# Single-chunk blocks at the start of a recurrence that is interleaved with a mixture of experts, and first weights in two tiles

## The chip, the cores and the metric

One core of one Trainium2 chip, fp32 throughout. The metric is the device time of one execution in microseconds (us). The median of three runs of the kernel before was 1271.88 us (1271.21 to 1275.32).

## The reference

A recurrence over 768 steps for 4 x 8 heads of width 40, whose output is the input of a mixture of four experts for every token.

```python
for t in range(S):                       # S = 768, state is (B, H, 40, 40)
    y[:, :, t] = einsum('bhd,bhde->bhe', r_t, state)
    Sa = einsum('bhde,bhe->bhd', state, a_t)
    state = state * w_t[:, :, None, :] - einsum('bhd,bhe->bhde', Sa, b_t)
    state = state + einsum('bhd,bhe->bhde', v_t, k_t)
x = y.transpose(0, 2, 1, 3).reshape(B * S, H * D)      # 3072 tokens x 320
p = domain_probs / domain_probs.sum(-1, keepdims=True)
out = sum(p[:, e:e + 1] * (relu(x @ w1[e]) @ w2[e]) for e in range(4))   # 320 -> 1024 -> 320
```

## The kernel before: the parts that matter

The 768 steps are 12 chunks of 64. Chunks are grouped into blocks: [0], then [1,2], [3,4] and so on to [9,10], then [11]. Within a block the recurrence is made parallel: both halves of the batch are prepared (transposes, running products, the `pef` products), one solve on VectorE inverts all small triangular systems of the block at once, then a chain of small products gives the block's output `Yo`. `AE` is the operand that VectorE prepares for `pef`; `pi` and `px` are the first products after the solve and need its results F and XT; `py` are the last ones before `Yo`. The mixture of a finished block is put into a queue of pieces, and TensorE works on those pieces in the gaps of the next block's recurrence. TensorE's order is fixed by the program: a call `mix(n)` stands where pieces may run, and the `credit` spreads the queue over the block.

```python
def mix(us):
    credit[0] += us * credit[1]
    while queue and credit[0] >= queue[0][0] / 2:
        t, piece = queue.pop(0)
        credit[0] -= t
        piece()

def attention(b, after):
    for p in range(NP):
        ...                                    # prepare half p, up to the pef products
        mix((22, 12)[p])
        ...
        mix(4.3)
        ...
    solve()                                    # VectorE; its last steps write F, then XT
    ...
    mix(40)                                    # pieces meant to run during the solve
    for x in range(2):
        for u in us:
            last = inverse(u, x)               # pi needs F, px needs XT
        ...
        mix(4.3)
    ...                                        # the chain to py and Yo, with more mix calls

for y, b in enumerate(all_blocks):
    credit[:] = [0.0, (sum(t for t, _ in queue) - 17) / 124]
    attention(b, ...)
    credit[:] = [sum(t for t, _ in queue) - 17, 1.0]
    mix(0)                                     # 17 us of pieces are left for the next block
    queue += mixture(b.cs, b.xT)
```

A piece is `wide` (hidden units: `ph` products, then ReLU on ScalarE) or `narrow` (`po` products, then a weighted sum into `osb` on VectorE).

```python
def mbank(name):
    return ps.tile([P, 512], FP32, name=name, tag="mbank", bufs=4)

def wide(e, f):
    ph = [mbank("ph") for _ in range(2)]
    ...
def narrow(e, tt):
    po = mbank("po")
    ...                                        # 8 products of 320 columns
    nc.vector.scalar_tensor_tensor(            # tensor_scalar for the first expert
        out=osb[tt][:], in0=po[:, 0:DM], scalar=sc, in1=osb[tt][:], op0=ALU.mult, op1=ALU.add)
```

The order of VectorE's instructions is chosen by the tile framework's scheduler when the kernel is built, except where `tc.issue_after` ties it.

## Time and profile before

The tables below cut the trace at the moments where the second `Yo` of a block starts. "Idle" is wall less busy time of TensorE (PE).

| stage of the kernel before | until | wall us | PE busy | PE idle |
|---|---|---|---|---|
| block [0] | 84.5 | 84.5 | | |
| block [1,2] | 226.8 | 142.3 | 108.6 | 33.7 |
| block [3,4] | 419.2 | 192.4 | 184.6 | 7.8 |
| the rest | 1270.0 | 850.8 | 823.3 | 27.5 |

From block [3,4] on TensorE is the bound; before, it often waits for VectorE.

### The profile page before, as it was taken

How to read it: one execution, taken by the hardware profiler on the slowest of the kernel's cores; microseconds unless marked ns; L12 is line 12 of the kernel's file. 1: busy time of each engine (PE TensorE's matmuls, PEld its weight loads, DVE VectorE, ACT ScalarE, POOL GpSimd, SP SyncE). 2: the span in 40 equal slices, each digit the busy share in tenths (PEclk: the TensorE clock that was granted, in tenths of full speed). 3: DMA queues.
4: the chain of work that ended last, by engine and by line, in shares of the span. 5: the costliest groups of instructions: out<-in, count | busy, mean ns of one | idle time of the engine just before them, and what ended most of it. 6: DMA issues, size and time to landing. Idle time of an engine off the chain costs nothing.

```text
span 1270.0 us, 28505 instructions
## 1 busy us (share of the span) xinstructions
PE 1153.0 (91%) x12736; PEld 785.1 (62%) x12736; DVE 710.6 (56%) x953; ACT 277.7 (22%) x588; POOL 80.4 (6%) x120
## 2 busy tenths in 40 slices
PE   3268679989999998999998999998999999999998
PEld 2256658756567656567656557655558656566776
DVE  7979865878513868604778704569903546601000
ACT  2112332032141032141122141122231212131111
POOL 5000000100000000000000000000000000000110
PEclk9768779998999998999998999998999999999999
DMA  6537444874323574333555424465314472232453
GB/s 135 126 84 156 105 105 96 179 178 102 98 49 95 120 176 108 86 84 95 119 151 107 114 63 103 99 165 112 93 46 86 110 160 49 77 84 74 120 150 93
DMA packets 164633, 138.21 MB, mean 109 GB/s; under 512 B 78688, under 2 KB 148384, under 8 KB 164512
## 3 DMA queue, kind: packets, MB, share of 16 engines
q0 software_dynamic: 17600, 73.46, 23.2%
q1 hardware_dynamic: 144192, 62.13, 22.6%
q8 instruction: 100, 1.64, 0.6%
q10 hardware_dynamic: 2720, 0.82, 0.3%
q14 instruction: 21, 0.17, 0.0%
HBM read 128.50 MB, written 7.86 MB: 107 GB/s over the span
## 4 chain that ended last, share of the span: by engine, by line
PE 66%; DVE 21%; DMA 6%; issue 4%; SPq 1%; ACT 1%; DVEq 0%; POOL 0%; ACTq 0%
PE po L594 24%; PE ph L582 24%; DVE KNT L209 3%; DVE GI L259 3%; PE py L496 2%; PE pc L484 2%; DMA out_dram<-osb 2%; PE pef L294 2%; PE pVST L429 2%; PE py L524 2%; PE pt L468 2%; DVE AT L209 2%; DVE tmp L360 2%; PE pa L458 2%; PE pSN L429 1%
## 5 line engine op out<-in xcount | busy, mean ns | idle before, releaser
L582 PE MATMUL ph<-xT,w1s 64*128 64x512 f32 (+1 forms) x2240 | 437.1, 538 | 11.5 <-DMA xT<-yD 8.1
L594 PE MATMUL po<-w2s,hs 128*128 128x320 f32 x1536 | 434.9, 443 | 0.5 <-ACT hs L588 0.5
L594 PEld LDWEIGHTS po<-w2s,hs 128*128 128x128 f32 x1536 | 294.1, 194 | 134.2 <-issue 20.2
L582 PEld LDWEIGHTS ph<-xT,w1s 64*128 64x128 f32 x2240 | 221.2, 190 | 198.4 <-issue 182.7
L588 ACT ACTIVATE hs<-ph 128x512 f32<-128x512 f32 (+1 forms) x224 | 110.1, 534 | 625.4 <-PE ph L582 624.8
L603 DVE SCALAR_TENSOR_TENSOR osb<-po,gate,osb 128x320 f32<-128x320 f32 x72 | 38.5, 547 | 218.1 <-PE po L594 217.9
L259 DVE RECIPROCAL GI<-G 128x512 f32<-128x512 f32 x24 | 78.6, 3309 | 0.1
L568 POOL DMA_DIRECT2D w1s<-in_moe_w_dram x56 | 37.8, 679 | 628.1 <-PE ph L582 628.0
L475 DVE TENSOR_SCALAR VS__98<-pt 64x320 f32<-64x320 f32 x12 | 5.8, 481 | 121.8 <-PE pt L468 121.8
L301 ACT COPY F<-pef 32x512 f32<-32x512 f32 x96 | 45.1, 470 | 110.6 <-PE pef L294 109.2
L572 POOL DMA_DIRECT2D w2s<-in_moe_w_dram x28 | 26.0, 928 | 532.9 <-PE po L594 525.5
L294 PE MATMUL pef<-AE__111,KNT 40*64 40x64 f32 x640 | 20.3, 310 | 31.9 <-DVE AE__111 L277 31.9
L435 DVE COPY VST<-pVST 128x512 f32<-128x512 f32 x24 | 16.6, 692 | 46.4 <-PE pVST L429 46.3
L294 PE MATMUL pef<-AE__110,KNT 40*64 40x64 f32 x896 | 18.8, 240 | 24.1 <-DVE AE__110 L277 24.1
L294 PEld LDWEIGHTS pef<-AE__111,KNT 40*64 40x64 f32 x640 | 18.8, 218 | 35.0 <-issue 35.0
L360 DVE TENSOR_TENSOR tmp<-Y,Tl 128x1024 f32<-128x1024 f32 (+2 forms) x49 | 35.7, 729 | 1.7
L406 PE MATMUL pi<-F 32*32 32x32 f32 x768 | 15.6, 203 | 23.1 <-DVE F L383 23.1
L364 DVE TENSOR_REDUCE Xl<-tmp 128x32 f32<-128x128 f32 (+3 forms) x49 | 35.5, 725 | 1.7
L364 DVE TENSOR_REDUCE Y<-tmp 128x32 f32<-128x256 f32 (+3 forms) x49 | 35.5, 725 | 1.7
L294 PEld LDWEIGHTS pef<-AE__110,KNT 40*64 40x64 f32 x896 | 17.0, 152 | 29.6 <-DVE AE__110 L277 22.6
L315 PE MATMUL pkn<-ident,KNT 128*128 128x128 f32 x192 | 30.0, 303 | 3.8 <-DVE AE__110 L303 3.1
L490 DVE TENSOR_TENSOR CX<-pc,mask 128x512 f32<-128x512 f32 x48 | 29.9, 684 | 6.1 <-PE pc L484 6.1
(120 smaller groups left out, 1050.7 us busy)
## 6 DMA issues: line engine op xcount, KB each, us to landing
w1s<-in_moe_w_dram POOLq DMA_DIRECT2D x56, 640.0 KB, 8.3
w2s<-in_moe_w_dram POOLq DMA_DIRECT2D x28, 1280.0 KB, 7.2
xT<-yD SPq DMA_DIRECT2D x24, 320.0 KB
yD<-Yo SPq DMA_DIRECT2D x48, 80.0 KB
out_dram<-osb SPq DMA_DIRECT2D x48, 80.0 KB
nat__76<-in_w_dram SPq DMA_DIRECT2D x16, 160.0 KB
nat__76<-in_a_dram SPq DMA_DIRECT2D x16, 160.0 KB
nat__74<-in_r_dram SPq DMA_DIRECT2D x16, 160.0 KB
```

The lines of the kernel that those rows point to most:

```text
L209: nc.vector.transpose(out=out.rearrange("p c m (r q) -> p m q c r", q=nq), in_=n[:, Q:Q + end].rearrange("p (m q e) -> p m q e", q=nq, e=D ...
L259: last = nc.vector.reciprocal(out=b.GI[:, c], in_=b.G[:, c, :, 1:L + 1])
L294: nc.tensor.matmul(out=pef[s][half(x), m * L:(m + 1) * L], lhsT=KNT[rows(s), m, x, :], rhs=u.AE[rows(s), s, m, :], start=True, stop=True,)
L301: nc.scalar.copy(out=F_[r, u.m, 0:L - z * Q], in_=cut(pef[s][r])[:, :, z * Q:L])
L360: nc.vector.tensor_tensor(out=m, in0=in0[:, :, None, :].to_broadcast([P, n0, n1, nr]), in1=in1[:, None, :, :].to_broadcast([P, n0, n1, nr] ...
L364: nc.vector.tensor_reduce(out=out, in_=m, axis=AX.X, op=ALU.add, negate=negate)
L429: nc.tensor.transpose(out=p[:, j * P:(j + 1) * P], in_=t[:, i, j].rearrange("p s d -> p (s d)"), identity=ident[:],)
L568: nc.gpsimd.dma_start(out=w1s[half(d)], in_=moe_w1[e, :, d * (F // 2):(d + 1) * (F // 2)].rearrange("(k p) f -> p k f", p=64),)
L582: nc.tensor.matmul(out=ph[d][:, 0:n], lhsT=w1s[half(d), k_, f * P:(f + 1) * P], rhs=xT[half(d), k_, 0:n], start=(k_ == 0), stop=(k_ == NK ...
L588: nc.scalar.activation(out=hs[-1][1][:, 0:n], in_=ph[d][:, 0:n], func=ACTF.Relu)
L594: nc.tensor.matmul(out=po[:, 0:DM], lhsT=h[:, tt * P:(tt + 1) * P], rhs=w2s[:, f, :], start=(x == 0), stop=(x == NF - 1),)
L603: nc.vector.scalar_tensor_tensor(out=osb[tt][:], in0=po[:, 0:DM], scalar=sc, in1=osb[tt][:], op0=ALU.mult, op1=ALU.add,)
```

## The change

The idle time of TensorE is in the first blocks, where there is little mixture to fill it. With single chunks at the start, [0], [1], [2], the mixture of chunk 1 is ready earlier and can fill block [2]. A larger part of the queue (30 us for 17) is carried into the first block of two. The first expert weights `w1s` are held in two tiles of half the columns each, so that one can be refilled earlier. Chunk 0's clearing of `XT` is remembered as the end of the solve for VectorE's order.

```diff
             if by is nc.vector:
-                by.memset(XT[o, :, 0:Q], 0.0)
+                last = by.memset(XT[o, :, 0:Q], 0.0)
 ...
+        return last.ins
 ...
-            w1s = wts.tile([P, NK, F // 2], FP32, name="w1s", tag="w1s", bufs=1)
+            w1s = [wts.tile([P, NK, F // 4], FP32, name=f"w1s{x}", tag=f"w1s{x}", bufs=1) for x in range(2)]
 ...                                # four DMAs of half the columns for two
-            mix((22, 12)[p])
+            mix(((11, 8), (22, 12))[b.n - 1][p])
 ...
-            cleared(nc.vector)
+            solved.append(cleared(nc.vector))
 ...
-    all_blocks = [block(cs) for cs in [[0]] + [[c, c + 1] for c in range(1, NC - 1, 2)] + [[NC - 1]]]
+    all_blocks = [block(cs) for cs in [[0], [1], [2]] + [[c, c + 1] for c in range(3, NC - 1, 2)] + [[NC - 1]]]
 ...
-        credit[:] = [0.0, (sum(t for t, _ in queue) - 17) / 124]
+        left = 17 if y + 1 == len(all_blocks) or all_blocks[y + 1].n <= b.n else 30
+        credit[:] = [0.0, (sum(t for t, _ in queue) - left) / (85, 124)[b.n - 1]]
 ...
-        credit[:] = [sum(t for t, _ in queue) - 17, 1.0]
+        credit[:] = [sum(t for t, _ in queue) - left, 1.0]
```

More of the change, by code (lines that the diff above doesn't have):

```diff
@@ L392, in cleared @@
             if by is nc.vector:
-                by.memset(XT[o, :, 0:Q], 0.0)
+                last = by.memset(XT[o, :, 0:Q], 0.0)
             else:
-                by.copy(out=XT[o, :, 0:Q], in_=zero[o, None, :].to_broadcast([Q, 2 * NP * M, Q]))
+                last = by.copy(out=XT[o, :, 0:Q], in_=zero[o, None, :].to_broadcast([Q, 2 * NP * M, Q]))
+        return last.ins
     def inverse(u, x):
@@ L560, in weights @@
         def weights(e):
-            w1s = wts.tile([P, NK, F // 2], FP32, name="w1s", tag="w1s", bufs=1)
+            w1s = [wts.tile([P, NK, F // 4], FP32, name=f"w1s{x}", tag=f"w1s{x}", bufs=1) for x in range(2)]
             w2s = wts.tile([P, NF, DM], FP32, name="w2s", tag="w2s", bufs=1)
             if cs[0] == e == 0:
-                for t in (w1s, w2s):
+                for t in w1s + [w2s]:
                     nc.gpsimd.tensor_copy(out=t[:, 0, 0:1], in_=all_blocks[0].units[1].KNT[:, 0, 0, 0:1])
-            for d in range(2):
-                nc.gpsimd.dma_start(
-                    out=w1s[half(d)],
-                    in_=moe_w1[e, :, d * (F // 2):(d + 1) * (F // 2)].rearrange("(k p) f -> p k f", p=64),
-                )
+            for x in range(2):
+                for d in range(2):
+                    o = (2 * d + x) * (F // 4)
+                    nc.gpsimd.dma_start(
+                        out=w1s[x][half(d)], in_=moe_w1[e, :, o:o + F // 4].rearrange("(k p) f -> p k f", p=64),
+                    )
             nc.gpsimd.dma_start(out=w2s[:], in_=moe_w2[e].rearrange("(f p) d -> p f d", p=P))
@@ L582, in wide @@
                     nc.tensor.matmul(
-                        out=ph[d][:, 0:n], lhsT=w1s[half(d), k_, f * P:(f + 1) * P], rhs=xT[half(d), k_, 0:n],
+                        out=ph[d][:, 0:n], lhsT=w1s[f // 2][half(d), k_, f % 2 * P:(f % 2 + 1) * P], rhs=xT[half(d), k_, 0:n],
                         start=(k_ == 0), stop=(k_ == NK - 1),
```

## The prediction

> **What bounds the kernel now.** I read the page first (busy shares, slices), then the table of busy time by stretch, with the stretches cut where VectorE starts a new block, then TensorE's waits in the first stretches, then the timeline of the second block.
>
> ```profile
> PE   3268679989999998999998999998999999999998
> DVE  7979865878513868604778704569903546601000
> PEclk9768779998999998999998999998999999999999
> ```
>
> TensorE is full from slice 7 on (a slice is 31.75 us); VectorE is full before that. The table says how much there is to win (columns: wall, then busy us of PE, PEld, DVE, ACT, POOL, then granted clock, DMA share, GB/s):
>
> ```profile
> 0.00:88.00 88.00, 36.42 (x752) 32.86 (x752) 72.47 (x117) 14.91 (x32) 18.90 (x39) 0.84 0.51 109
> 88.00:236.00 148.00, 117.57 (x1878) 97.96 (x1880) 109.95 (x143) 36.61 (x86) 6.83 (x9) 0.82 0.53 119
> 236.00:430.00 194.00, 186.48 (x2102) 123.31 (x2099) 115.30 (x147) 47.30 (x98) 10.47 (x14) 0.97 0.49 117
> 430.00:624.00 194.00, 185.07 (x2072) 120.61 (x2072) 111.23 (x145) 43.85 (x90) 7.75 (x10) 0.98 0.45 106
> ```
>
> Rows: block [0], block [1,2], then two of the four full blocks of two. PE is idle 51.6 us in [0], 30.4 in [1,2], 8 to 9 in each later one. Block [1,2] has only the mixture of chunk 0 to fill TensorE with, and runs at a granted clock of 0.82. The change aims there. TensorE's waits in 88:236 and the timeline name the cause:
>
> ```profile
> PE pef L294 <- DVE AE__111 L277: 13.2, 2, 12.5
> PE pi L406 <- DVE F L383: 8.8, 1, 8.8
> PE ph L582 <- DMA xT<-yD: 8.1, 2, 7.7
> ```
> ```profile
> 92.20 1.19 PE L582 MATMUL ph<-xT,w1s 64*128 64x256 f32 x2 [7.74 <-DMA xT<-yD]
> 106.21 0.33 PE L294 MATMUL pef<-AE__110,KNT 40*64 40x64 f32 x4 [1.39 <-DVE AE__110 L277]
> 135.83 0.48 PE L294 MATMUL pef<-AE__111,KNT 40*64 40x64 f32 x4 [12.46 <-DVE AE__111 L277]
> 175.54 3.62 PE L406 MATMUL pi<-F 32*32 32x32 f32 x128 [8.75 <-DVE F L383]
> ```
>
> So block [1,2] is a VectorE chain: ready at 89.2, first half prepared at 106.2, second at 135.8, solve done at 175.5; then a mixed chain to the last py product at 226.7. The same landmark of block [3,4] is 419.1. After that every block is bound by TensorE with about 17 us of mixture left over, before and after the change alike. **The whole question is whether the last py of [3,4] comes before or after 419.1.**
>
> **What the Trainium skill says.** "TensorE: Matmul & The Clock Gate", Part 1: a TensorE idle for about 3.4 us falls to half clock, and needs as long to recover. The trace agrees: the 16 po products at 110.3 took 7.05 us, 4.47 at 118.9. "VectorE: DVE Perf Modes", The TRN2 errata: each instruction pays a fixed latency, so two small ones cost more than a large one. It agrees for products (686 ns for 512 columns, 1220 for 1024), not for transposes (about 690 ns for 512, 1980 for 1024): one-chunk blocks have the cheaper transposes. "DMA: Bandwidth & Descriptors", Anatomy of one DMA: about 2 us plus bytes/436 GB/s, so 1280 KB would be some 5 us; this trace has 7.2 to 8.3 us to landing. The trace decides.
>
> **The change part by part.**
>
> *Costs added.* One more block means one more solve: 31.0 to 64.9 in block 0, 33.9 us of VectorE whatever the block's size. It means one more pass over the expert weights (73.46 MB / 7 = 10.5 MB). And 512 columns of mixture become two times 256: a ph group of 20 costs 2.36 us at 256 against 4.35 at 512, so 16 x (4.72 - 4.35) = 6 us, plus group edges; I use 8.
>
> *Block 0* gets shorter: the clears of XT go ahead of the R transposes (about 1 us of the pt wait), and the next decay is one chunk, not two (transpose 0.71 for 1.97, scans 1.2 for 2.3), in the way of the VS copies. I take 2 us: VectorE free at 87.2, xT at 90.2.
>
> *Block [1].* The queue counts a wide piece at 2.15 and a narrow one at 4.3, 68.8 in all, so (68.8-17)/85 = 0.61 us of mixture per unit. 11 units: 3 wide pieces, cold, 10 us, to 100.2 (the AE is ready near 96). pef 2, a wide and a cold narrow piece 9.4, pkn 1.1: 112.8; the second AE is ready at about 112 (masks 4, GI 3.3, transposes 2.1, products 2 after the first). pef and masks to 118, R 0.7, solve to F 29.9 (block 0: 31.0 to 60.9), three osb rows 1.6: F at 150. TensorE has 35 us of work in that time: it fits. From F: pi and px 2.4, pt 2.1, VST to py 9.35 (192.5 to 201.85), mixture 17.2 x 0.61 x 1.07 = 11.2: last py at **175**.
>
> *Block [2].* VectorE: 4.8 after py (as 226.7 to 231.5), G 2.0, GI 3.3, transposes 2.1, products 1.9: pef at 189. TensorE has 11 x 0.66 x 1.07 = 7.7 us ready, so it waits 6. Second AE 12 later, 201; masks 4, R, solve and osb 32.2: F at 237.5; TensorE gets to it at 240. Tail 13.8 + 12.1: last py at **266**. So a one-chunk block takes 90 us, a VectorE chain again, against 78 to 82 us of TensorE work in it.
>
> *Block [3,4].* Its mixture is 68.8 + 30 carried, (98.8-17)/124 = 0.66 per unit; block [1,2] had (68.8-17)/124 = 0.42, the full blocks 1.11. So it is the former [1,2] over again: VectorE ready at 270.8, G 4.4, then 136.5 (89.3 to 226.7 less 0.9 for the gates): 411.7. More mixture after the solve: (0.66-0.42) x 34.4 x 1.07 = 8.9. A warmer TensorE gives back about 4 (pef 3.7 against 2.1, pi 3.6 against 2.2, VectorE's waits on them). Loads in the dense one-chunk blocks cost about 3 on VectorE's path: the fourth load is issued only after the gather. Last py: 411.7 + 8.9 - 4 + 3 = **419.6**, against 419.1.
>
> *Split w1s tile.* Waits on w1s are 2.0 us in all now (longest 0.8); it saves at most that, and mainly keeps the added 256-column mixtures from stalling: the first half can be refilled two wide pieces earlier.
>
> Sum: 1271.9 + 0.5 = 1272.4. The new constants (30, 11, 8, 85) look fitted on a chip, which is no measurement but makes me lean a little to gain: I say **1267 us**.
>
> **Rivals.**
> (1) *The idle time is really filled.* Then the 30 us idle and some 17 us of cold clock in [1,2] shrink to about 15 by the end of [3,4], less 8 for narrow mixtures and some waits: 15 to 25 us gained, 1250. For it: PE work fits the solve of [1] and [2] nearly exactly. Against: the carried 30 us is spread over 124 units, so the first 22 units of [3,4] give 15 us of work where VectorE needs 26; the 12 us holes stay.
> (2) *DMA becomes the bound of the one-chunk blocks.* 10.5 MB of weights and about 5 MB of the rest in 90 us is 172 GB/s, where [1,2] had 119 at a share of 0.53. I estimate a share of 0.75. w1s now lands in smaller packets. Each expert lasts about 22 us there, landing 8, so stalls should be small; but late A and W loads would sit straight on VectorE's chain: 1285 to 1295. For it: VectorE already waits 7 to 10 us at a time for loads behind out stores in later blocks, harmless there.
> (3) *The deficit only moves.* [3,4] inherits all of [1,2]'s waits and the extra solve eats the rest: 1272. This is my sum.
>
> **Range and chances.** Three errors of about 5 us each (blocks [1] and [2], block [3,4], loads), with the lean: predicted 1267, range 1250 to 1287. Faster by over 2% means below 1246, all of rival 1 and more: 0.06. Slower by over 2% means above 1297: 0.05. Within 2%: 0.89.
>
> **What would show each step.** Last py of [1], [2] and [3,4] near 175, 266 and 420; pef of [3,4] waiting about 10 us for AE twice; the wait for F near zero in [1] and [2]; no TensorE wait on w1s above 1 us; later blocks still 194 to 196 us each. VectorE stalls on loads of over 5 us in [1] or [2] would say rival 2; both pef waits of [3,4] under 5 us, rival 1. The prediction fails if the order of VectorE's instructions changes much (the second half's preparation slipping ahead of the first's masks, say), since the chain is then not the one I added up.

## The result

The changed kernel takes **1325.66 us** (median of 4 runs, 1323.22 to 1328.55), against 1273.6 (1271.21 to 1276.19) for the kernel before in the same rounds: ratio 1.0409, 95% interval 1.0376 to 1.0443. Ratios, here and below, are the mean time of one kernel's fast runs over that of the other's of the same rounds, so not quite the ratio of the medians. It is 4.1% slower, outside the predicted range of 1250 to 1287.

**Where the time went.** First the slices of the page of the kernel after (40 slices, now 33.1 us each), to be read against the PE line of before in the prediction:

```profile
PE   3278794877597999899999999999899999999998
```

Counted from 1, the last digit below 8 stands in slice 13, which ends at 430 us; in the kernel before it stands in slice 6, which ends at 190 us. The table of busy time by stretch for the kernel after, with the stretches [1], [2] and [3,4] (columns: window, wall, busy us of PE, PEld, DVE, ACT and POOL with counts, granted clock, DMA share, GB/s):

```profile
83.70:192.10 108.40, 85.11 (x1090) 68.93 (x1090) 67.30 (x108) 23.49 (x56) 10.81 (x15) 0.86 0.53 120
192.10:308.80 116.70, 87.88 (x1130) 71.24 (x1132) 68.70 (x106) 24.68 (x60) 12.18 (x17) 0.85 0.55 127
308.80:474.00 165.20, 132.68 (x2009) 108.73 (x2009) 109.66 (x138) 39.44 (x96) 15.75 (x22) 0.90 0.57 131
```

The same view of the kernel before, for [1,2] and [3,4]:

```profile
84.50:226.80 142.30, 108.62 (x1825) 91.34 (x1826) 104.42 (x136) 35.95 (x84) 5.90 (x8) 0.81 0.53 117
226.80:419.20 192.40, 184.62 (x2106) 124.67 (x2108) 113.66 (x146) 45.79 (x96) 10.05 (x13) 0.97 0.49 116
```

Chunks 1 to 4 take 390.3 us after and 334.7 before: 55.6 us more. TensorE's busy time in it rises from 293.2 to 305.7, its idle time from 41.5 to 84.6. What follows takes 851.0 us after and 850.8 before. So **the whole loss is made in chunks 1 to 4, three quarters of it as idle time**, and it is never won back.

TensorE's waits in that stretch (engine, line, waited for: us in total, times, longest) in the kernel after, then its two waits for AE in the same stretch of the kernel before (84.5 to 419.2); the prediction has the other waits of before:

```profile
PE pef L294 <- DVE AE__110 L277: 34.6, 7, 11.4
PE ph L584 <- DVE osb L603: 18.0, 3, 7.7
PE pef L294 <- DVE AE__111 L277: 11.9, 2, 11.1
PE ph L584 <- DMA xT<-yD: 7.7, 2, 7.3
PE ph L584 <- DVE osb L605: 7.2, 1, 7.2
```

```profile
PE pef L294 <- DVE AE__111 L277: 17.8, 4, 12.5
PE pef L294 <- DVE AE__110 L277: 2.3, 2, 1.4
```

The second and the last line of the first list are new (0.3 us in the kernel before): 25.2 us in which **the `ph` products wait for `osb` sums on VectorE**. The waits of `pef` for AE grow by as much again, from 20.1 to 46.5 us, and the wait for F (8.8 us before) is gone. The waits for `osb` come first here; those for AE come back with block [2] and with what stays open. The timeline of block [1] after shows how this comes about (start, duration, engine, line, what, count, and in brackets the wait before it):

```profile
138.72 8.88 PE L596 MATMUL po<-w2s,hs 128*128 128x320 f32 x32
147.53 2.43 PE L584 MATMUL ph<-xT,w1s 64*128 64x256 f32 x20
149.53 1.22 DVE L364 TENSOR_REDUCE Xl<-tmp 128x64 f32<-128x1024 f32 x1
150.79 1.90 DVE L383 STREAM_TRANSPOSE F<-Xl 128x1024 f32<-128x1024 f32 x1
152.55 4.14 DVE L385 STREAM_TRANSPOSE XT<-Xl 128x1024 f32<-128x1024 f32 x2
156.60 0.96 DVE L605 SCALAR_TENSOR_TENSOR osb<-po,gate,osb 128x320 f32<-128x320 f32 x2
157.17 6.48 PE L584 MATMUL ph<-xT,w1s 64*128 64x256 f32 x40 [7.21 <-DVE osb L605]
163.58 1.20 PE L407 MATMUL pi<-F 32*32 32x32 f32 x64
```

Follow it from the top. Two narrow pieces fill two of the four banks; their products end at 143 and 147.6. Their sums stand in VectorE's order behind the whole end of the solve, and run at 156.6 only. Meanwhile one more wide piece (20 `ph` products) takes the other two banks. The banks are handed out in turn, so the next wide piece needs the two that the sums still hold: TensorE stands still for 7.21 us. F, which `pi` needs, has been ready since 152.7 (150.79 + 1.90). But in TensorE's order the remaining mixture comes before `pi`, so that begins at 163.6: **10.9 us after F was there**. The Trainium skill ("PSUM — Partial Sum Buffer", section "Engine vs sequencer instructions") says that the other engines' queues are strictly first in, first out, and that matmuls run in program order; the trace agrees: the sums' operands were complete 9 us before VectorE came to them, and `pi` was ready for 10.9 us behind a stalled `ph`.

The same happens in [2], where `pi` comes 13.0 us after F:

```profile
272.82 8.61 PE L584 MATMUL ph<-xT,w1s 64*128 64x256 f32 x58 [6.79 <-DVE osb L603]
281.36 1.20 PE L407 MATMUL pi<-F 32*32 32x32 f32 x64
```

and in [3,4], where it comes 11.4 us after F. In the kernel before one of the two sums was placed just as late, and it cost nothing. Its timeline in [1,2]:

```profile
173.04 0.54 DVE L603 SCALAR_TENSOR_TENSOR osb<-po,gate,osb 128x320 f32<-128x320 f32 x1
173.50 1.90 DVE L383 STREAM_TRANSPOSE F<-Xl 128x1024 f32<-128x1024 f32 x1
175.25 4.19 DVE L385 STREAM_TRANSPOSE XT<-Xl 128x1024 f32<-128x1024 f32 x2
179.36 0.50 DVE L603 SCALAR_TENSOR_TENSOR osb<-po,gate,osb 128x320 f32<-128x320 f32 x1
```

There TensorE had no mixture left in front of `pi` and already stood waiting for F (the wait of 8.75 us that the prediction shows). The idle time that the change wanted to fill was the slack that hid VectorE's late sum.

Block [2] has a second trouble, at its beginning. VectorE's timeline after:

```profile
208.60 0.71 DVE L209 STREAM_TRANSPOSE AT<-nat__75 128x512 f32<-128x512 f32 x1 [4.24 <-DMA nat__75<-in_a_dram]
215.32 0.69 DVE L209 STREAM_TRANSPOSE R<-nat__76 128x512 f32<-128x512 f32 x1
221.77 0.55 DVE L605 SCALAR_TENSOR_TENSOR osb<-po,gate,osb 128x320 f32<-128x320 f32 x1 [5.75 <-PE po L596]
222.23 0.70 DVE L209 STREAM_TRANSPOSE G<-nat__76 128x512 f32<-128x512 f32 x1
```

Here the coupling runs the other way: a sum stands before the preparation of the second half, and VectorE waits 5.75 us for TensorE's `po`. The second half's `pef` comes at 232.3, 22.1 us after the first's at 210.2.

### The profile page after: what moved, and what is told of

Its sections match the earlier page's. It is cut to its first block, busy times and chain, and to the rows that moved or that the text cites. A ratio compares the mean times of both kernels' runs of the same rounds, so it can differ in the third digit from the quotient of the medians.

```text
span 1325.0 us, 29527 instructions
## 1 busy us (share of the span) xinstructions
PE 1162.4 (88%) x13056; PEld 823.2 (62%) x13056; DVE 735.8 (56%) x1023; ACT 282.7 (21%) x624; POOL 132.1 (10%) x197
## 4 chain that ended last, share of the span: by engine, by line
PE 63%; DVE 23%; DMA 7%; issue 4%; SPq 1%; ACT 1%; DVEq 0%; ACTq 0%
PE po L596 23%; PE ph L584 23%; DVE tmp L360 3%; DVE GI L259 2%; PE py L497 2%; PE pt L469 2%; PE pef L294 2%; PE pc L485 2%; PE py L525 2%; PE pVST L430 2%; DVE KNT L209 2%; DVE Y L364 2%; DVE Xl L364 2%; DVE AT L209 1%; PE pd L505 1%
## 5 line engine op out<-in xcount | busy, mean ns | idle before, releaser
L584 PE MATMUL ph<-xT,w1s 64*128 64x256 f32 (+1 forms) x2560 | 442.7, 496 | 35.0 <-DVE osb L603 18.0
L584 PEld LDWEIGHTS ph<-xT,w1s 64*128 64x128 f32 x2560 | 255.6, 192 | 197.7 <-issue 148.6
L590 ACT ACTIVATE hs<-ph 128x256 f32<-128x256 f32 (+1 forms) x256 | 112.6, 488 | 655.7 <-PE ph L584 655.3
L571 POOL DMA_DIRECT2D w1s<-in_moe_w_dram x128 | 85.7, 674 | 641.5 <-PE ph L584 605.0
L294 PEld LDWEIGHTS pef<-AE__110,KNT 40*64 40x64 f32 x1024 | 23.4, 172 | 63.7 <-issue 38.9
L364 DVE TENSOR_REDUCE Y<-tmp 128x32 f32<-128x256 f32 (+3 forms) x56 | 40.6, 724 | 1.9
L530 DVE TENSOR_TENSOR Yo<-py,G 128x512 f32<-128x512 f32 x24 | 16.2, 690 | 38.9 <-PE py L525 38.6
L303 DVE TENSOR_TENSOR AE__110<-pef,mask 64x512 f32<-64x512 f32 x32 | 22.0, 689 | 26.3 <-ACT F L301 25.8
L385 DVE STREAM_TRANSPOSE XT<-Xl 128x1024 f32<-128x1024 f32 x16 | 33.5, 2140 | 0.0
L497 PE MATMUL py<-R,SN 40*64 40x64 f32 x768 | 27.6, 225 | 6.2 <-issue 6.2
```

What stands on the lines that cost most here:

```text
L294: nc.tensor.matmul(out=pef[s][half(x), m * L:(m + 1) * L], lhsT=KNT[rows(s), m, x, :], rhs=u.AE[rows(s), s, m, :], start=True, stop=True,)
L364: nc.vector.tensor_reduce(out=out, in_=m, axis=AX.X, op=ALU.add, negate=negate)
L497: nc.tensor.matmul(out=py[half(s), m * L:(m + 1) * L], lhsT=SN[rows(s), i, j * P + s * 64:j * P + (s + 1) * 64], rhs=u.R[rows(s), m, :], s ...
L571: nc.gpsimd.dma_start(out=w1s[x][half(d)], in_=moe_w1[e, :, o:o + F // 4].rearrange("(k p) f -> p k f", p=64),)
L584: nc.tensor.matmul(out=ph[d][:, 0:n], lhsT=w1s[f // 2][half(d), k_, f % 2 * P:(f % 2 + 1) * P], rhs=xT[half(d), k_, 0:n], start=(k_ == 0), ...
L590: nc.scalar.activation(out=hs[-1][1][:, 0:n], in_=ph[d][:, 0:n], func=ACTF.Relu)
```

## The experiments

My theory after the comparison: the sums on VectorE, placed behind the solve's end, hold PSUM banks and stop TensorE, and through its order delay `pi` (theory A; the expectations call it theory 1, the loads rival 2 and the added solve rival 3). The rivals: the added expert loads (DMA) delay the one-chunk blocks; the added solve and the narrower products cost as much by themselves, whatever the order; the carried amount of 30 is wrong; the split `w1s` costs something. Twelve kernels ran, on three chips in groups of four, each with the kernel before in the same rounds.

### e1_oldblocks: the small parts without the blocks

```diff
-[[0], [1], [2]] + [[c, c + 1] for c in range(3, NC - 1, 2)] + [[NC - 1]]
+[[0]] + [[c, c + 1] for c in range(1, NC - 1, 2)] + [[NC - 1]]
-        left = 17 if y + 1 == len(all_blocks) or all_blocks[y + 1].n <= b.n else 30
+        left = 17
```

> The change without its new blocks and without the larger carry: blocks of 1,2,2,2,2,2,1 as before, with the two column tiles for the first weights and the clears ordered ahead. If the loss lies in the one-chunk blocks (my theory, and the rival of the extra weight loads as well), this runs like the kernel before or up to 3 us faster: 1268 to 1275 us. If the split tile itself costs (twice as many GpSimd-issued loads of half the size), it is slow too, 1290 us or more.

Measured 1274.97 us, before 1275.37: ratio 1.0005 (0.9959 to 1.005). The split tiles and the clearing cost nothing and gain nothing that can be measured. The loss is in the blocks, with the larger carry that only they use (e7 tries that alone).

### e2_pool and e3_pool_before: the sums taken off VectorE, in the kernel after and in the kernel before

```diff
             if e == 0:
                 osb.append(mo.tile([P, DM], FP32, name="osb", tag="osb", bufs=4))
-                nc.vector.tensor_scalar(out=osb[tt][:], in0=po[:, 0:DM], scalar1=sc, ...)
+                nc.scalar.mul(out=osb[tt][:], in_=po[:, 0:DM], mul=sc)
             else:
-                nc.vector.scalar_tensor_tensor(out=osb[tt][:], in0=po[:, 0:DM], scalar=sc, in1=osb[tt][:], ...)
+                pot = mo.tile([P, DM], FP32, name="pot", tag="pot", bufs=1)
+                nc.scalar.mul(out=pot[:], in_=po[:, 0:DM], mul=sc)
+                nc.gpsimd.tensor_add(osb[tt][:], osb[tt][:], pot[:])
```

> The changed kernel, with the mixture's sums taken off VectorE: ScalarE scales po out of its PSUM bank, GpSimd adds. Theory 1 (in blocks [1], [2] and [3,4] the osb sums stand behind the tail of the solve in VectorE's order, hold two of the four PSUM banks, and TensorE stands still with mixture ahead of pi): TensorE's waits on osb (25 us in these blocks) vanish, pi follows F within 3 us (13, 13 and 11 us late now), and the time falls by 30 to 45 us, to 1280 to 1297. Rival 2 (the extra pass over the weights and the denser loads hold these blocks) and rival 3 (the extra solve of 34 us itself): it stays above 1315.

> Control for the one above: the same move of the sums in the kernel before. TensorE waits there on osb for only 3 us in all, so theory 1 says 1265 to 1275 us: the move gains little where no bank is held. If it gains 25 us or more here too, the move is a gain of its own and the run above doesn't speak for theory 1.

e2 took 1280.59 us (ratio to before 1.005, 0.9994 to 1.0106), e3 1256.27 (0.9871, 0.9813 to 0.9928). e2 is within what theory A expected, at its lower end. The move is worth 45 us in the kernel after and 19 in the kernel before. I had expected less of e3 (1265 to 1275). The table by stretch for e2, again [1], [2], [3,4]:

```profile
87.20:187.60 100.40, 84.02 (x1090) 68.24 (x1090) 64.67 (x103) 26.45 (x62) 15.25 (x19) 0.87 0.58 129
187.60:287.80 100.20, 86.65 (x1130) 69.88 (x1132) 65.92 (x100) 27.61 (x66) 15.83 (x21) 0.91 0.65 148
287.80:441.50 153.70, 132.13 (x2009) 108.17 (x2010) 106.85 (x130) 44.04 (x105) 22.67 (x29) 0.90 0.60 140
```

Chunks 1 to 4 take 354.3 us for 390.3. The waits of `ph` for `osb` are gone from TensorE's list; in their place one wait for F is back:

```profile
PE pef L294 <- DVE AE__110 L277: 24.1, 6, 9.5
PE pef L294 <- DVE AE__111 L277: 10.4, 2, 9.7
PE pi L407 <- DVE F L383: 4.2, 1, 4.2
```

In e3, chunks 1 to 4 take 334.8 us, as in the kernel before (334.7): there the move gains nothing in this stretch, as theory A says, and its 19 us come later (832.3 us for 850.8 after [3,4]; what makes them was not tested). So the pair says two things. The sums on VectorE cost the kernel after 36 us in chunks 1 to 4 and the kernel before none. And with the sums out of the way in both, the new blocks still lose 19.5 us there (354.3 against 334.8), of which 9.6 are TensorE's busy time (302.8 against 293.2) and 9.9 its idle time. Theory A is the larger part, not the whole.

### e4_osbfirst: the sums ahead of the solve's last transposes

The mixture pieces of the solve are traced before it (TensorE's order stays the same), and the transpose into F is tied behind the last sum.

```diff
+        ahead = b.cs[0] in (1, 2, 3)
+        if ahead:
+            mix(40)                          # narrow() leaves its last sum in added[0]
-        solve()
+        solve(added[0] if ahead else None)
 ...
-        nc.vector.transpose(out=columns(F_), in_=X)
+        with tc.issue_after(first) if first else ExitStack():
+            nc.vector.transpose(out=columns(F_), in_=X)
```

> The changed kernel, with only VectorE's order changed: in blocks [1], [2] and [3,4] the osb sums that wait behind the solve's last three transposes (about 6 us) are put ahead of them. TensorE's order is the same, nothing is added or removed. Theory 1: TensorE goes on about 5 us earlier in each of the three blocks, F comes 1 us later, so 10 to 16 us less: 1309 to 1316. Rivals 2 and 3: no change, 1322 to 1330.

Measured 1321.74 us (1.0366, 1.0311 to 1.042), not told apart from the kernel after (1.0409): a miss. The trace of VectorE in [1] says why:

```profile
154.87 4.22 DVE L386 STREAM_TRANSPOSE XT<-Xl 128x1024 f32<-128x1024 f32 x2
158.99 0.97 DVE L606 SCALAR_TENSOR_TENSOR osb<-po,gate,osb 128x320 f32<-128x320 f32 x2
159.87 1.92 DVE L384 STREAM_TRANSPOSE F<-Xl 128x1024 f32<-128x1024 f32 x1
```

I had tied F alone, so the scheduler pulled XT ahead of the sums. Counted from the end of [0] (87.30 here, 83.67 there), they came only 1.2 us earlier than in the kernel after, and F came 5.5 us later. The edit did not make the order that I meant, and says nothing against the theory.

### e5_osbmid: the sums ahead of the last part of the solve

As e4, but the tie is on the second half of the solve's last products and reductions, 2.5 us before F's transpose (`last_` marks the last call of `dots`).

```diff
                 for x in (slice(0, n0 // 2), slice(n0 // 2, n0)):
-                    dots(out[:, x], in0[:, x], in1, negate)
+                    with tc.issue_after(first) if last_ and x.start and first else ExitStack():
+                        dots(out[:, x], in0[:, x], in1, negate)
```

> The run before this with that name of purpose (osb sums ahead of the transposes) missed its aim: VectorE put the two XT transposes ahead of the sums and F behind them, so the sums came only 2 us earlier and F 5 us later. Here the edge is on the last reduce of the solve: in blocks [1], [2] and [3,4] the two sums stand ahead of that reduce and of all three transposes, about 7 us earlier than in the changed kernel, F 1 us later; TensorE's order is the same. Theory 1 (the bank held until the sums are done): TensorE's waits on osb in the three blocks fall from 25 to 8 us or less and the time by 15 to 24 us, to 1301 to 1311. Rivals 2 and 3 (loads, the solve's length): 1322 to 1330.

Measured **1297.01 us** (1.0153, 1.0122 to 1.0184): 29 us less than the kernel after by the medians, or 33 by the difference of the two ratios (0.0256 of 1275 us), and below what I had expected. The timeline in [1], where block [0] happened to end 3.2 us later than after's:

```profile
142.37 8.88 PE L597 MATMUL po<-w2s,hs 128*128 128x320 f32 x32
151.18 6.75 PE L585 MATMUL ph<-xT,w1s 64*128 64x256 f32 x60
151.81 1.00 DVE L606 SCALAR_TENSOR_TENSOR osb<-po,gate,osb 128x320 f32<-128x320 f32 x2
153.98 1.22 DVE L365 TENSOR_REDUCE Xl<-tmp 128x64 f32<-128x1024 f32 x1
155.23 1.96 DVE L384 STREAM_TRANSPOSE F<-Xl 128x1024 f32<-128x1024 f32 x1
157.86 1.20 PE L408 MATMUL pi<-F 32*32 32x32 f32 x64
```

The same two sums, the same engine, the same duration; they only stand before the last reduction, 8.0 us earlier than in the kernel after, counted from the end of [0] (151.81 - 86.88 against 156.60 - 83.67). TensorE's 60 `ph` products now run without a stop, and `pi` follows F's end by 0.7 us instead of 10.9. In [2] it follows by 2.3 us, in [3,4] by 0.7. TensorE's waits in chunks 1 to 4:

```profile
PE pef L294 <- DVE AE__110 L277: 31.8, 7, 10.2
PE pef L294 <- DVE AE__111 L277: 10.6, 2, 9.8
PE ph L585 <- DMA xT<-yD: 8.1, 2, 7.7
PE ph L585 <- DVE osb L604: 2.3, 1, 2.3
```

The `osb` waits fall from 25.2 to 2.3 us, and chunks 1 to 4 from 390.3 to 357.1: 33.2 us by order alone, with the same work on the same engines. By block it is 10.3, 12.3 and 10.6 us. The two traces' lists of VectorE instructions differ in this stretch only in where these two sums of each block stand (compared line by line), and the stretch repeats well: e8, with the order of the kernel after, takes 389.0 us. Theory A is shown, for this much. The waits for AE stay (42.4 us for 46.5), so they are another matter. The second half of [2] still came 22.1 us after the first (`pef` at 200.4 and 222.4), with VectorE waiting 5.7 us for `po` as before; I had not tied that sum.

### e6_fewloads: the rival of the loads

In the mixtures of chunks 0 to 2 all experts use the weights of the first, which takes 9 of 12 passes of loads out of exactly the stretch in question. The result is wrong (relative error 0.767).

```diff
-            if f == 0:
+            if f == 0 and (e == 0 or len(cs) > 1 or cs[0] > 2):
                 weights(e)
+            elif f == 0:
+                w[e] = w[e - 1][:2] + ([],)
```

> The changed kernel, wrong on purpose: the mixtures of chunks 0, 1 and 2 load only expert 0's weights and use them for all four experts, so that 9 of the 12 loads of weights (23.6 MB) in this part are gone; the orders of VectorE and TensorE are the same. Theory 1: only the wait on the fourth load (4.2 us in block [2]) can go: 1318 to 1326. Rival 2 (the extra pass over the weights): 1300 or less.

Measured 1316.48 us (1.0323, 1.0287 to 1.036). The table for [1], [2] and [3,4]:

```profile
82.50:187.30 104.80, 83.10 (x1090) 67.03 (x1090) 67.32 (x108) 23.46 (x56) 0.00 (x0) 0.87 0.24 49
187.30:303.40 116.10, 90.65 (x1130) 73.74 (x1132) 68.72 (x106) 24.84 (x60) 3.61 (x5) 0.84 0.36 78
303.40:471.00 167.60, 136.99 (x2009) 112.52 (x2009) 109.61 (x138) 39.50 (x96) 3.60 (x5) 0.87 0.35 79
```

The DMA share falls from 0.53 to 0.57 down to 0.24 to 0.36, and chunks 1 to 4 still take 388.5 us for 390.3. The loads are not the main cause. Most of the timed gain of some 9 us lies in what follows (844.3 us for 851.0), whose program is the same; I can't explain it.

### e7_left17: the carried amount

```diff
-all_blocks[y + 1].n <= b.n else 30
+all_blocks[y + 1].n <= b.n else 17
```

> The changed kernel with 17 us of mixture carried everywhere, in place of 30 into the first block of two. It also shifts VectorE's order: in blocks [2] and [3,4] both sums now stand within the solve, not behind it. Theory 1: the waits on osb in these two blocks (10.3 and 7.7 us) shrink to under 5 together, 10 to 18 us less: 1308 to 1316, although less is carried. If the carry is what matters and not the order: block [3,4] has 13 us less to fill its holes with, 1326 to 1338.

Measured 1334.22 us (1.0452, 1.0426 to 1.0478), a little above the kernel after (1.0409, with intervals that overlap), where I had expected a gain; in the trace chunks 1 to 4 take 399.6 us for 390.3. [2] takes 130.8 us for 116.7, [3,4] 160.5 for 165.2. TensorE's wait for `osb` near the solve's end in [2] did fall, from 6.8 to 4.7 us, but 13 us less carried is 13 us more mixture in block [2], and all of it ran in front of `pi`:

```profile
269.74 1.93 DVE L383 STREAM_TRANSPOSE F<-Xl 128x1024 f32<-128x1024 f32 x1
290.61 1.20 PE L407 MATMUL pi<-F 32*32 32x32 f32 x64
```

`pi` now starts 19 us after F. That supports the second half of theory A: what hurts is anything that stands before `pi` in TensorE's order when F is ready. In [3,4] the expectation came true: both sums now stand inside the solve (at 409.4 and 413.5, F's transpose at 420.2), and `pi` comes 3.1 us after F instead of 11.4.

### e8_onetile: the split undone in the kernel after

The `w1s` part of the change is reversed, all else stays.

> The changed kernel with the first weights in one tile, loaded in halves by columns of two tiles' width as before; VectorE's order is the same. The chunks' mixtures of 256 columns are short, so the refill shows: 2 to 10 us slower than the changed kernel, 1327 to 1336. If the 72 more loads issued by GpSimd cost more than they hide, it is faster, under 1322.

Measured 1328.97 us (1.0408, 1.0382 to 1.0434; the kernel after, 1.0409), not the 2 to 10 us more that I had expected. Waits on `w1s` came back in chunks 1 to 4, but only 2.9 us of them. The split is worth nothing here, as e1 said for the old blocks.

### e9_shortsolve: a shorter solve, with the sums off VectorE

e2 with the last stage of the solve left out in [1] and [2], some 15 us of VectorE each. The arithmetic is wrong; the result still passed the tolerance, which says only that this stage matters little for these inputs.

```diff
-        for n in (8, 16):
+        for n in (8,) if short else (8, 16):
 ...
-        solve()
+        solve(b.cs[0] in (1, 2) and b.n == 1)
```

> The changed kernel with the sums off VectorE, and, wrong on purpose, blocks [1] and [2] without the last stage of their solve: 15 us less of VectorE's chain in each. If the extra solve is what is left of the loss (that kernel stands some 23 us behind the kernel before with its sums off VectorE as well), the time falls by 20 to 30 us, to 1250 to 1260. My reading of its trace is that TensorE reaches pi 3 us behind F in [1] and waits for F only 4 us in [2], because its mixture fills the solve: then at most 3 to 8 us fall away, 1272 to 1278, and the rest of the loss is the two preparations of each block, the 12 us of additional TensorE time and the late half-clock products.

Measured 1266.86 us (0.9939, 0.9908 to 0.997): 14 us less than e2, for 30 us less of VectorE; in the trace chunks 1 to 4 take 345.6 us, 8.7 less than in e2. This lies between the two expectations. The trace shows what holds the rest back, in [1]:

```profile
134.67 1.95 DVE L383 STREAM_TRANSPOSE F<-Xl 128x1024 f32<-128x1024 f32 x1
146.87 6.75 PE L584 MATMUL ph<-xT,w1s 64*128 64x256 f32 x60
153.54 1.20 PE L407 MATMUL pi<-F 32*32 32x32 f32 x64
```

F is ready at 136.6, and TensorE is still busy, without a wait, with the mixture that the program puts before `pi`, until 153.5. So once the sums are out of the way, VectorE and TensorE hold block [1] almost alike: with 15 us of VectorE taken away it takes 98.6 us for 100.4, because TensorE holds it. Less work on TensorE was not tried.

### e10_left45: more carried, with the sums off VectorE

e2 with 45 for 30.

> The changed kernel with the sums off VectorE, carrying 45 us of mixture into the first block of two, not 30. The run with 17 carried was 5 us slower than the changed kernel, against what I expected: the carry is worth more than I had reckoned. If more carried fills the holes of [3,4] (10 us waits for AE), it is 3 to 10 us faster than with 30: 1270 to 1278. If block [2] then stands idle instead, because its 100 us are set by VectorE, there is no change: 1278 to 1286.

Measured 1277.29 us (1.0034, 0.998 to 1.0088), not told apart from e2 (1.005). [2] takes 91.8 us for 100.2, [3,4] 166.3 for 153.7: what [2] saves, [3,4] pays. This is the prediction's third rival, in one pair of blocks.

### e11_m_left17: e5 with 17 carried

> The order mended as in the run that put the sums ahead of the last reduce, with 17 carried, not 30. It separates the carry from VectorE's order, which changed together in the earlier run with 17. If the carry alone is worth some 10 us: 1303 to 1313, against 1297 with 30. If the earlier loss came from the order: 1292 to 1300.

Measured 1331.86 us (1.0457, 1.0421 to 1.0494). Inconclusive: with more mixture in [2], my tie made VectorE wait for two of TensorE's `po` in the middle of the solve (14.25 and 3.75 us, ahead of F), so the edit changed two things. Neither expectation came true. It shows only that the tie of e5 fits 30 carried and not 17.

### e12_pool_split: the old blocks with the sums off VectorE

e1 with the move of e2, looking for a version that beats both.

> The best of both: the blocks of the kernel before, its sums off VectorE, with the split first weights and the clears ahead. The kernel before with its sums off VectorE took 1256 us, with 2.0 us of waits on w1s: 1252 to 1258.

Measured 1257.77 us (0.987, 0.9835 to 0.9905), the same as e3 (0.9871): 1.3% faster than the kernel before, 5% faster than the kernel after. The interval lies clear of 1. The old blocks with the sums off VectorE are the best version found.

## Why the prediction was wrong, point by point

The predicted last `py` of [3,4] was 419.6, measured 474.0: 54.4 us, and with it the whole error of its sum (1272.4). The step from there to 1267 was a lean that rested on no measurement, as the prediction says, and added 5 us; what happened had been given a chance of 0.05. Set beside the prediction's landmarks, with F meaning the end of its transpose:

| term of the sum | predicted | measured | error |
|---|---|---|---|
| end of [0] | 82.5 | 83.7 | +1.2 |
| [1]: from the end of [0] to F | 67.5 | 69.0 | +1.5 |
| [1]: from F to `pi` | 0 | 10.9 | **+10.9** |
| [1]: from `pi` to the end | 25 | 28.5 | +3.5 |
| [2]: from the end of [1] to F | 62.5 | 76.2 | **+13.7** |
| [2]: from F to `pi` | 2.5 | 13.0 | **+10.5** |
| [2]: from `pi` to the end | 26 | 27.4 | +1.4 |
| [3,4]: from F to `pi` | 0.1, as before | 11.4 | **+11.3** |
| [3,4]: all else | 153.5 | 153.9 | +0.4 |

(The 82.5 is the prediction's "2 us shorter" taken off 84.5.)

**The step that failed** is the one in block [1]: "TensorE has 35 us of work in that time: it fits." It compared two amounts, the mixture and the solve's duration, and took it that a piece runs whenever TensorE is free. But a narrow piece needs VectorE for its sum, and a bank until that is done; VectorE was in the middle of a solve and took the sums after it. The work fits in amount and not in order. [2] and [3,4] inherited the step, so it stands three times in the table: 32.7 us in all. e5 removes it by order alone, and chunks 1 to 4 get 33.2 us shorter. The two figures come from different traces, and agree.

**The second error is a size**, in block [2]: "Second AE 12 later, 201". It was 22.1 us, because a sum of the old mixture stands before the second half's preparation and VectorE waits for TensorE's `po` (5.75 us), and because R, G, a scan and two sums lie on the way that I had not counted; that is 10 of the 13.7 us, and a late load of A, of which the prediction spoke under rival 2, is 4. In e2, without sums on VectorE, the second AE comes 15.4 us after the first (201.4 to 216.8). I had carried over a distance from block [1] without looking up which sums would stand in it.

**What was right.** The post-solve chains (errors of 1.4 to 3.5 us) and F in block [1] (1.5 us). `pef` of [3,4] waited 10.2 and 11.1 us for AE, predicted about 10 twice. No wait on `w1s` and no gain from its split (e1, e8). The later blocks were unchanged (851.0 us for 850.8). The landmark logic held: the time did come from the end of [3,4] alone. And the failure was named in the condition at the end, "if the order of VectorE's instructions changes much": the order mattered, although it had hardly changed; what changed was that TensorE had work waiting behind it.

**A reading to correct.** The prediction takes the slow `po` products at 110.3 as agreement with the clock rule that it cites. They did run at half clock, but TensorE's waits just before them were 1.39 and 0.92 us, not 3.4. A cleaner place in the same trace agrees only for the fall: TensorE stops at 84.5, the granted clock reads 0.50 from 88.0, work begins again at 92.2, and the clock is back at 98.2, after 6.0 us of work.

**The rivals.** Rival 1 (the holes are filled) failed for the same reason as the sum. Rival 2 (DMA) is refuted as the main cause by e6; its mark was a VectorE stall on loads of over 5 us, and the longest in these two blocks was 4.24. Rival 3 (the deficit moves) is visible in e10.

**What stays open.** With the sums off VectorE in both kernels, the new blocks still cost 24 us by the medians (1280.59 against 1256.27), 19.5 of it in chunks 1 to 4. About half is more busy time of TensorE; I had counted 8 for narrower products, less 4 for a warmer clock, and it was 9.6. The other half is idle time, mostly waits of `pef` for AE, in the first half of each block: 34.5 us in e2, 18.3 in e3. e9, which takes away about as much VectorE time (30 us) as the added solve brought (34), won 8.7 us in this stretch: 7.6 of them busy time of TensorE (302.8 to 295.2), 1.1 idle. So the solve has a part, and with TensorE's order as it is not the whole. A clean split I do not have.

## What to carry to other kernels

Before filling an engine's idle time with work, follow one piece of that work to the instruction that frees its buffer, and look where that instruction stands in the other engine's order: if that engine is in its long serial section, the work will stop when the buffers are full, and everything behind it in program order stops with it. A late release that costs nothing in the old profile may be hidden by the very idle time that the change wants to use. When the sums that release such buffers are small, an engine with room (here ScalarE, busy for 278 of 1270 us in the kernel before, and GpSimd) can take them; in e2 the waits of `ph` for `osb` were then gone.

## What the Trainium skill lacked or had wrong

- "PSUM — Partial Sum Buffer" gives the order of the queues, and collisions, but nothing on what a shared ring of banks does when its release stands late in another engine's queue. Here, with four banks shared by two kinds of piece, sums of 0.5 us each, placed behind the solve's end and not before its last part (8 us later in the first block), cost 33.2 us over three blocks.
- "DMA: Bandwidth & Descriptors", section "Anatomy of one DMA": as an estimate, its fit of 2 us plus bytes over 436 GB/s gives 2.8 us for a load of 320 KB and 3.5 us for one of 640 KB; the medians from issue to landing in these runs are 5.0 us (128 loads of the kernel after) and 8.3 us (56 loads of the kernel before), each into 64 partitions and with other traffic on the queues; which of the two makes the difference was not tested.
- "Perfetto Trace Analysis" lacks the case in which moving work off VectorE pays because of where the work stands in VectorE's order, and not because VectorE is full: it is busy for 56% of the kernel after. In e2 ScalarE's multiply of 128x320 took 0.53 us and GpSimd's add 0.86 us in the median (up to 1.83), for 0.55 us of VectorE, and the kernel became 45 us faster.
